# The first half of w_in split later in the head of a linear-attention plus gated-MLP kernel

## Chip, cores and metric

One NeuronCore of a Trainium2 chip runs the whole program; inputs and output lie in HBM. The metric is device microseconds of one execution, the median of several executions. Engines: TensorE (PE), with its weight loads shown apart (PEld); VectorE (DVE); ScalarE (ACT); GpSimd (POOL); SyncE (SP), which only issues DMAs here.

## What is computed

Batch 4, 4 heads of 32, sequence 1088, so a model width of 128; the MLP is 1024 wide and is cut into halves u and v of 512.

```python
q_p, k_p = phi(q), phi(k)            # phi: outer product of two 8-wide projections
kv = einsum('bhsf,bhsd->bhfd', k_p, v); z = k_p.sum(axis=2)
x = (q_p @ kv) / (q_p @ z + 1e-6)    # heads side by side: [B, S, 128]
h = gelu(x @ w_in); u, v = h[..., :512], h[..., 512:]
v_n = layernorm(v) * g_ln
v_s = einsum('ts,bsd->btd', w_sg, v_n) + b_sg[None, :, None]
out = x + (u * v_s) @ w_out
```

`w_in`, `w_out` and S come as 64-bit floats; the chip splits their words into two 32-bit parts itself.

## The kernel before

**Precision.** Most products are made as three matmuls in a 32-bit format that rounds its operands, of a high and a low part of each: high by high, low by high, high by low. So nearly every operand is first copied to a rounded high part (ACT) and then subtracted from itself for the low part (DVE).

**Stages of a batch.** Attention gives x (tiles `x_h`, `x_l`). Then, per 128 rows t of the 9 row tiles: `v1`/`v2` (L746 to L755) multiply x by the second half of `w_in`; `gelu` (L760); mean and variance, for tiles 0 to 2 by `mean`/`sq` on ACT, for the others by `bn` (L776, L777) on DVE; `norm`, a chain of some ten small DVE instructions (L793 to L822); `v3` (L828, ACT) normalizes; `vh` (L838, ACT) and `vl` (L843, DVE) split. The spatial product `z` (L851, L860) sums over t, for 4 blocks db of 128 channels and 3 column parts ci: `zh` is the two matmuls with the high part of W (`w_h`), `zl` the one with its low part (`w_l`). `pu` (L875 to L877) is three matmuls of x by the first half of `w_in`, `ug` (L882) its gelu into u; then `gt`, `gm`, `gh`, `gl`, `po` gate it and multiply by `w_out`.

**The head.** Batch 0 starts with nothing in place, so its stages are written out one by one. While q, k and v arrive, PE makes the features of batch 0 in three column parts c: `qe`, `qm0` (L630), `k2` (L436), `q03` (L650), `den1`, `den2`, `xt` (L668), a transpose `tr` (L686), then `x1` (ACT, L689) and `x2` (DVE, L693) write a third of `x_h`, `x_l`. `fill` steps are matmuls without use (L675). The words of `w_in` are split by `split64` (L241 to L256) in eight steps 0 to 7 per half; `wi1` is the second half (for v), `wi0` the first half (for u). Of `wi0`, step 0 (L241) and 7 (L256, writes `win_h`) run on ACT; 1 (L242), 2 (L245), 3 (L248), 4 (L249), 5 (L250) and 6 (L251, writes `win_l`) on DVE. `wo` is the same for `w_out`; its step 0 (`woa`, L241) waits for the load `raw_out`. `wlo` (L719) subtracts the high part of W from `w_f` for the low one.

**What sets the order.** Every piece of work is a named step. A list `WHEN` of 1773 numbers, written out in the file, gives each step a place; the steps are emitted sorted by place, and each engine runs its own instructions strictly in the order in which they were emitted, with waits on semaphores where the data need them. A step's DMAs go into the queue of the engine that issues it: SP for `load`, POOL for `ld_wh` and `wd`. `gate_wf` (L309) is a one-column POOL copy that reads a chunk of `w_h` and writes into `w_f0`, so that the loads of `w_f` begin only when that chunk of `w_h` has landed.

**Buffers.** `new(shape, tag, name)` takes a place in a ring per tag: tag "x" has 4 (`raw_win1`, `raw_win0`, `x_h`, `x_l`, later `w_f7`, `raw_out`), tag "w" has 8 (`w_f0` to `w_f6`, then the `w_l`). `bank` takes one of 8 PSUM banks; six of them hold z of two channel blocks while the head runs.

Of the kernel before, what the change touches and what calls it, by code (L numbers as in the profile page):

```python
# [9 lines left out]
I64 = mybir.dt.int64  # L10
# [6 lines left out]
P = 128  # L17
# [3 lines left out]
DG = 512  # L21
# [16 lines left out]
HALVES = ((0, 1), (1, 2), (3, 2), (5, 1), (6, 3))  # L38

WHEN = [  # L40
# [111 lines left out]
def tile_kernel(tc, qd, kd, vd, sd, wd, bd, wind, woutd, q0d, vid, outd, pool, dram, psum):  # L152
# [9 lines left out]
    def new(shape, tag, name, dt=F32):  # L162
        return pool.tile(shape, dt, tag=tag, name=name, bufs=BUFS.get(tag, 1))
# [4 lines left out]
    T = {}  # L168
# [140 lines left out]
        G.tensor_copy(w_f(0)[:, :1], f32(T["w_h"][:, HALVES[-2][0], :1]))  # L309

    def load_win(i):
        T["raw_win", i] = new([P, DG], "x", f"raw_win{i}", I64)
        load(T["raw_win", i], wind[:, DG * i : DG * i + DG])

    def load_wout():
# [24 lines left out]
    for p in (1, 0):  # L340
        at(("ld_v0", p), lambda p=p: load_v0(p))
    at("ld_win1", lambda: load_win(1))
    at("ld_win0", lambda: load_win(0))
    at("gate_wh", gate_wh)
    for t, n in HALVES:
# [717 lines left out]
    class Sums:  # L1063
# [28 lines left out]
        def load(self, i):  # L1092
            n, t, k, tag, at = self.PARTS[i]
            if at // 3 not in self.raw:
                self.raw[at // 3] = new([P, 3, WP], "kld", f"wr{at // 3}")
            load(self.of(i), self.d[n][:, t : t + k])
# [322 lines left out]
```

## Time and profile before

| | us |
|---|---|
| runs of the kernel | 319.04, 320.27, 321.16 |
| their median | 320.27 |
| the execution that was profiled | 319.73 |
| its span, first to last instruction | 317.7 |

So 2.0 us of the profiled execution lie around the span. The granted TensorE clock is 1.000 over the span. In the views below a start is in microseconds from the start of the span. A matmul's row gives start and duration; matmuls overlap, so what one costs in a stream is the distance from one start to the next. "x4" is a number of instructions, the arrow a releaser.

### The profile page before, as it was taken

The numbers are of one execution on the slowest core, as the hardware profiler recorded it, in microseconds if no ns is written. First come the engines' busy times: TensorE is split into PE (matmuls) and PEld (weight loads), VectorE is DVE, ScalarE is ACT, GpSimd is POOL, SyncE is SP. The second block draws the span as 40 slices with busy tenths as digits, with TensorE's granted clock in tenths as the row PEclk, the third lists the DMA queues.
The fourth block names the chain that finished last, engine by engine and source line by source line (L and its number), as shares of the span: only waits on it lengthen the run. The fifth ranks groups of instructions, "written<-read, shape, count | busy, mean of one in ns | idle before, by whom it ended". The sixth has DMA issues, their size and how long they took to land.

```text
span 317.7 us, 6545 instructions
## 1 busy us (share of the span) xinstructions
PE 310.8 (98%) x2510; PEld 298.3 (94%) x2510; DVE 271.5 (85%) x654; ACT 163.0 (51%) x360; POOL 35.8 (11%) x52
## 2 busy tenths in 40 slices
PE   7999999999999999999999999999999999999995
PEld 5777999999999999999999999999999999999995
DVE  5899999999998977799798877399888988889675
ACT  4589733556558743454646682345357753334321
POOL 0300000022220001023200002042030000000000
PEclk9999999999999999999999999999999999999999
DMA  6999972556474235642654055724093202510002
GB/s 219 349 425 370 405 313 98 111 123 143 152 172 136 39 109 155 146 129 28 103 94 95 0 153 122 180 66 150 2 200 93 76 18 83 147 47 3 0 0 70
DMA packets 19774, 42.27 MB, mean 133 GB/s; under 512 B 2176, under 2 KB 14624, under 8 KB 19328
## 3 DMA queue, kind: packets, MB, share of 16 engines
q1 hardware_dynamic: 14784, 27.17, 29.6%
q0 software_dynamic: 4960, 14.70, 17.3%
q8 instruction: 19, 0.31, 0.4%
q14 instruction: 11, 0.09, 0.1%
HBM read 35.87 MB, written 8.94 MB: 141 GB/s over the span
## 4 chain that ended last, share of the span: by engine, by line
PE 90%; DVE 6%; DMA 2%; SPq 1%; issue 0%; ACT 0%; DVEq 0%
PE pz L851 33%; PE pz L860 15%; PE pz L1050 5%; PE pu L875 3%; PE pu L877 2%; PE pu L876 2%; PE pv L755 2%; PE pv L747 2%; PE pv L746 2%; PE po L924 2%; PE po L921 2%; PE po L922 2%; DMA vn<-in_q 2%; PE pkv L436 1%; PE pk L404 1%; PE pnd L537 1%
## 5 line engine op out<-in xcount | busy, mean ns | idle before, releaser
L851 PE MATMUL pz<-w_h,vl 128*128 128x362 f32 (+1 forms) x324 | 105.3, 325 | 0.4 <-DVE vl L843 0.4
L851 PE MATMUL pz<-w_h,vh 128*128 128x362 f32 (+1 forms) x324 | 105.3, 325 | 0.0
L860 PE MATMUL pz<-w_l,vh 128*128 128x362 f32 (+1 forms) x288 | 87.5, 325 | 0.0
L851 PEld LDWEIGHTS pz<-w_h,vl 128*128 128x128 f32 x324 | 60.8, 188 | 2.2 <-DVE vl L843 1.2
L851 PEld LDWEIGHTS pz<-w_h,vh 128*128 128x128 f32 x324 | 60.8, 188 | 1.1
L860 PEld LDWEIGHTS pz<-w_l,vh 128*128 128x128 f32 x288 | 53.1, 188 | 0.3
L882 ACT ACTIVATE u<-pu 128x362 f32<-128x362 f32 (+1 forms) x48 | 22.5, 472 | 19.9 <-PE pu L877 12.4
L760 ACT ACTIVATE vn<-pv 128x512 f32<-128x512 f32 x36 | 21.0, 599 | 17.2 <-PE pv L755 16.8
L828 ACT ACTIVATE vn<-vn,nm,rs 128x512 f32<-128x512 f32 x36 | 28.7, 814 | 1.8 <-DVE nm L822 1.4
L888 DVE SCALAR_TENSOR_TENSOR gt<-pz,vi,b_bc 128x362 f32<-128x362 f32 (+3 forms) x41 | 23.5, 581 | 6.1 <-PE pz L851 5.5
L900 ACT CAST gh<-gt 128x362 fp32r<-128x362 f32 (+1 forms) x47 | 22.5, 492 | 12.0 <-DVE gt L895 7.5
L903 DVE TENSOR_TENSOR gl<-gt,gh 128x362 fp32r<-128x362 f32 (+1 forms) x47 | 24.5, 529 | 3.3 <-PE po L922 1.7
L895 DVE TENSOR_TENSOR gt<-gt,u 128x362 f32<-128x362 f32 (+3 forms) x49 | 25.7, 535 | 0.5 <-ACT u L882 0.2
L843 DVE TENSOR_TENSOR vl<-vn,vh 128x128 fp32r<-128x128 f32 (+1 forms) x54 | 22.3, 422 | 3.6 <-ACT vh L838 3.4
L838 ACT CAST vh<-vn 128x128 fp32r<-128x128 f32 (+1 forms) x54 | 20.4, 404 | 8.1 <-PE pz L851 7.7
L776 DVE BATCH_NORM_STATS2 st<-vn 128x6 f32<-128x512 f32 x33 | 22.4, 680 | 1.6 <-ACT vn L760 1.4
L550 DVE RECIPROCAL den<-den 128x362 f32<-128x362 f32 (+1 forms) x9 | 21.7, 2412 | 2.0 <-ACT den L545 1.8
L1050 PE MATMUL pz<-w_h,wb 128*128 128x364 f32 x64 | 19.2, 325 | 0.0
L529 POOL TENSOR_TENSOR qpl<-e_0a,qph 128x362 fp32r<-128x362 f32 x6 | 6.3, 1058 | 107.3 <-ACT qph L524 81.2
L545 ACT ACTIVATE den<-pnd,mask 64x362 f32<-64x362 f32 (+1 forms) x18 | 10.1, 560 | 13.6 <-PE pnd L538 13.4
L875 PE MATMUL pu<-x_h,win_h 128*128 128x362 f32 (+1 forms) x48 | 15.9, 331 | 0.0
L877 PE MATMUL pu<-x_l,win_h 128*128 128x362 f32 (+1 forms) x48 | 15.7, 327 | 0.0
(330 smaller groups left out, 635.8 us busy)
## 6 DMA issues: line engine op xcount, KB each, us to landing
w_f<-in_w SPq DMA_DIRECT2D x9, 576.0 KB
wt<-in_w POOLq DMA_DIRECT2D x6, 768.0 KB, 8.5
w_h<-in_w POOLq DMA_DIRECT2D x2, 1152.0 KB, 8.9
vi<-in_v SPq DMA_DIRECT2D x7, 306.0 KB
w_h<-in_w POOLq DMA_DIRECT2D x1, 1728.0 KB, 14.6
k<-in_k SPq DMA_DIRECT2D x3, 576.0 KB
wt<-wt POOLq DMA_DIRECT2D x2, 768.0 KB, 4.7
out<-o SPq DMA_DIRECT2D x8, 181.0 KB
```

What stands on the lines that cost most here:

```text
L776: V.bn_stats(st, self.vn[:, t])
L828: A.activation(self.vn[:, t], self.vn[:, t], AF.Identity, bias=self.nm[:, t : t + 1], scale=self.rs[:, t : t + 1])
L843: V.tensor_sub(vl[:, ts], self.vn[:, ts, P * db : P * db + P], f32(vh[:, ts]))
L851: mm(self.z[db, ci], lhsT=self.parts[db][i][:, t], rhs=T["w_h"][:, t, AT[ci] : AT[ci] + cw], start=(t == 0 and i == 0), stop=(t == NT - 1 ...
L860: mm(self.z[db, ci], lhsT=self.parts[db][0][:, t], rhs=T["w_l", t][:, AT[ci] : AT[ci] + CH[ci][1]], start=False, stop=False,)
L875: mm(pu, lhsT=T["win_h"][:, ws], rhs=xh[:, cs], start=True, stop=False)
L882: A.activation(self.u[db, ci], self.pu.pop((db, ci)), AF.Gelu_apprx_tanh)
L888: V.scalar_tensor_tensor(self.gt[db, ci][:, s], self.z[db, ci][:, s], T["g_col"][:, db : db + 1], T["b_bc"][:, c0 : c0 + cw][:, s], op0=AL ...
L895: V.tensor_mul(gt, gt, self.u[db, ci][:, s])
L900: A.copy(self.g[db, ci][0], self.gt[db, ci])
L903: V.tensor_sub(self.g[db, ci][1], self.gt.pop((db, ci)), f32(self.g[db, ci][0]))
L1050: mm(self.z[db, ci], lhsT=w[:, i, t % 4], rhs=r[:, cs], start=(t == 0 and q == 0), stop=False)
```

## The change

One line of code and the first third of `WHEN` change. The raw words of the first half (`raw_win0`) take a place in the ring "w" in place of one in "x":

```diff
     def load_win(i):
-        T["raw_win", i] = new([P, DG], "x", f"raw_win{i}", I64)
+        T["raw_win", i] = new([P, DG], "x" if i else "w", f"raw_win{i}", I64)
         load(T["raw_win", i], wind[:, DG * i : DG * i + DG])
```

```diff
 WHEN = [
-    1, 7, 2, 0, 5, 6, 8, 10, 15, 18, 21, 24, 56, 59, 66, 72, 76, 80, 35, 38, 9, 12, 14, 11, 13, 16, 17, 19, 20, 22,
+    1, 7, 2, 0, 5, 6, 8, 10, 15, 18, 21, 24, 56, 59, 66, 93, 97, 102, 35, 38, 9, 12, 14, 11, 13, 16, 17, 19, 20, 22,
...
```

The lists were sorted to see the order they make. Places 0 to 66 and all from 522 on hold the same steps in the same order; those between are permuted. No step is added or taken out, and no instruction of one changes. Places of the steps that matter (before, after):

| step | before | after |
|---|---|---|
| `wi0` 0, 1, 2, 3 | 103, 105, 109, 118 | 98, 113, 117, 127 |
| `wi0` 7, 4, 5, 6 | 115, 130, 116, 137 | 238, 247, 257, 276 |
| `pu` and `ug` of (db 0, ci 0) | 150, 158 | 319, 354 |
| `pu` and `ug` of (0, 1) | 172, 202 | 365, 402 |
| `pu` and `ug` of (0, 2) | 214, 217 | 290, 320 |
| `pu` of (1, 0) | 218 | 282 |
| first `zh` (0, 2, t 0), (0, 0, t 0), (0, 1, t 0) | 209, 211, 205 | 186, 187, 205 |
| `bn` 3, 4, 5 | 196, 178, 206 | 191, 190, 182 |
| `vl` of t 0 | 204 | 185 |
| `x1` of c 1, c 2; `gelu` 5 | 129, 175; 194 | 135, 164; 159 |
| `v1` 3, 6, 7, 8 | 136, 181, 183, 189 | 165, 166, 179, 192 |
| `v2` 3, 6, 7, 8 | 156, 193, 197, 199 | 175, 178, 201, 198 |
| `ld_wh` 3, 5, 6; `gate_wf` | 72, 76, 80; 142 | 93, 97, 102; 110 |
| `ld_w` 0; `ld_wout`; `ld_b`; `ld_v` of batch 1 | 145; 180; 201; 207, 210 | 114; 162; 281; 308, 324 |
| `wo` 0, `v3` 6, `vh` 6, `v3` 7, `vh` 7 | 275, 287, 291, 293, 299 | 251, 274, 291, 283, 285 |
| `zh` (0, 0, t 6) | 313 | 294 |
| `k1`, first `kf`, `k2` of batch 1 | 396, 410, 428 | 397, 411, 420 |

On SP the 124 DMAs stand in the same order before and after. On POOL two subtractions of batch 1 change places (`ql` 0 and 1), and nothing else does.

## Rows read from the trace of the kernel before

**Rows 1.** The page, part 1 (busy time) and part 4 (chain that ended last).
```profile
PE 310.8 (98%) x2510; PEld 298.3 (94%) x2510; DVE 271.5 (85%) x654; ACT 163.0 (51%) x360; POOL 35.8 (11%) x52
...
PE 90%; DVE 6%; DMA 2%; SPq 1%; issue 0%; ACT 0%; DVEq 0%
```

**Rows 2.** Busy time by stretch: PE, PEld, DVE, ACT, POOL, clock, DMA share, GB/s.
```profile
24.00:32.00 8.00, 7.55 (x38) 5.65 (x36) 7.59 (x36) 7.55 (x18) 0.68 (x1) 1.00 0.98 365
32.00:40.00 8.00, 8.00 (x50) 7.87 (x49) 7.46 (x29) 5.89 (x13) 0.00 (x0) 1.00 1.04 407
40.00:48.00 8.00, 8.00 (x50) 7.63 (x49) 8.00 (x11) 2.54 (x6) 0.00 (x0) 1.00 0.76 296
```

**Rows 3.** Timeline of PE at the first spatial products: start, duration, instruction, idle before.
```profile
28.06 0.33 PE L851 MATMUL pz<-w_h,vh 128*128 128x362 f32 x1
28.79 0.43 PE L851 MATMUL pz<-w_h,vl 128*128 128x362 f32 x1 [0.41 <-DVE vl L843]
...
33.07 0.32 PE L851 MATMUL pz<-w_h,vh 128*128 128x364 f32 x1
33.23 0.33 PE L851 MATMUL pz<-w_h,vl 128*128 128x364 f32 x1
```

**Rows 4.** Timeline of PE, 23 to 26 us: products for v, and u's between them.
```profile
22.71 0.40 PE L747 MATMUL pv<-win_l,x_h 128*128 128x512 f32 x1
22.94 0.39 PE L746 MATMUL pv<-win_h,x_h 128*128 128x512 f32 x1
...
24.92 0.33 PE L875 MATMUL pu<-x_h,win_h 128*128 128x362 f32 x1
25.09 0.33 PE L876 MATMUL pu<-x_h,win_l 128*128 128x362 f32 x1
25.26 0.33 PE L877 MATMUL pu<-x_l,win_h 128*128 128x362 f32 x1
25.57 0.50 PE L746 MATMUL pv<-win_h,x_h 128*128 128x512 f32 x1
```

**Rows 5.** Chain that ended last, 19 to 29 us: start, duration, what.
```profile
19.04 0.33 DVE wi0g L250
...
21.11 0.60 DVE wi0a L249
...
21.83 0.60 DVE win_l L251
...
25.87 0.61 DVE st L776
...
28.54 0.21 DVE vl L843
28.75 0.04 issue
28.79 1.08 PE pz L851 x5
```

**Rows 6.** Waits, 0 to 60 us: engine, line, what it waited for; total, times, longest.
```profile
POOL w_f L309 <- DMA w_h<-in_w: 9.9, 1, 9.9
...
ACT woa L241 <- DMA raw_out<-in_w_out: 1.6, 1, 1.6
```

**Rows 7.** Timeline of SP: DMA issues.
```profile
23.53 3.44 SPq L300 DMA_DIRECT2D w_f<-in_w  x5
27.09 0.42 SPq L317 DMA_DIRECT2D raw_out<-in_w_out  x1
```

**Rows 8.** Timelines of ACT from the landing of raw_out, and of DVE.
```profile
37.98 0.67 ACT L241 ACTIVATE woa<-raw_out 128x512 f32<-128x512 f32 x1 [1.55 <-DMA raw_out<-in_w_out]
38.55 0.82 ACT L828 ACTIVATE vn<-vn,nm,rs 128x512 f32<-128x512 f32 x1
39.40 0.30 ACT L838 CAST vh<-vn 128x128 fp32r<-128x128 f32 x1
39.60 0.81 ACT L828 ACTIVATE vn<-vn,nm,rs 128x512 f32<-128x512 f32 x1
...
38.15 0.29 DVE L843 TENSOR_TENSOR vl<-vn,vh 128x128 fp32r<-128x128 f32 x1
```

**Rows 9.** Timeline of PE round tile 6 of the first channel block.
```profile
43.06 0.32 PE L851 MATMUL pz<-w_h,vh 128*128 128x362 f32 x1
43.22 0.32 PE L851 MATMUL pz<-w_h,vl 128*128 128x362 f32 x1
43.38 0.32 PE L851 MATMUL pz<-w_h,vh 128*128 128x362 f32 x1
43.69 0.43 PE L851 MATMUL pz<-w_h,vl 128*128 128x362 f32 x1
43.96 0.33 PE L851 MATMUL pz<-w_h,vh 128*128 128x364 f32 x1
```

**Rows 10.** Timeline of PE: batch 1's keys, and the same for batch 2.
```profile
55.40 1.21 PE L404 MATMUL pk<-sk,k 128*32 128x64 f32 x72
56.54 0.43 PE L860 MATMUL pz<-w_l,vh 128*128 128x362 f32 x1
...
59.33 1.73 PE L436 MATMUL pkv<-vi,kp 128*32 128x34 f32 x144
60.99 0.43 PE L851 MATMUL pz<-w_h,vh 128*128 128x362 f32 x1
...
118.08 1.49 PE L436 MATMUL pkv<-vi,kp 128*32 128x34 f32 x144
```

**Rows 11.** Timeline of DVE, the features of batch 1's keys.
```profile
56.98 3.07 DVE L210 TENSOR_TENSOR kp<-pk,kb 128x256 f32<-128x256 f32 x9
```

**Rows 12.** Timeline of PE, first 20 us: the engine at its two clock levels.
```profile
0.94 3.25 PE L202 MATMUL warm<-ones 128*64 128x64 f32 x28 [0.94 <-POOL ones L194]
...
8.21 1.56 PE L610 MATMUL pn<-vn,sk 128*128 128x384 f32 x4 [0.86 <-DMA vn<-in_q]
9.31 2.19 PE L621 MATMUL pab<-qs,ex 128*128 128x384 f32 x8
```

78 rows, old and new, of the table WHEN are left out of this document.

## Prediction, made before the changed kernel was run

> **What bounds the kernel now.** Read first the busy shares and the chain that ended last: PE is busy for 98% of the span and 90% of that chain is PE's own work [rows 1]. The change takes no matmul away and adds none, so the time can move only by PE's gaps. The stretches say where these are: none of 8 us between 32 and 48, 0.45 us between 24 and 32, where DVE (7.59 of 8) and ACT (7.55) are as full as PE [rows 2]. A busy PE is not quite a streaming one, so the third view is PE's own timeline, read start to start. In a stream one matmul of 362 columns follows the next after 0.16 us (33.07 to 33.23); at the first spatial product it is 0.73 us (28.06 to 28.79), released by DVE's `vl`, so 0.57 us are lost there [rows 3]. Smaller losses stand at 43.4 us (0.31 and 0.27 us in place of 0.16, 0.26 us lost) [rows 9] and in the keys of batch 1: their 144 matmuls last 1.73 us, those of batch 2 last 1.49, so 0.24 us are lost [rows 10]. The named losses are 1.07 us together. What the change can win is of this order, and it has to be won twice: at the first spatial product, and at each later place where PE waits for something that does not depend on the head.
>
> **First place: what DVE no longer does before the first spatial product.** The chain up to it is DVE without a pause. Behind it go steps 4, 5 and 6 of `wi0`: 0.60, 0.33 and 0.60 us [rows 5], 1.53 us in all. Of the three `bn` steps before `vl`, two go behind and one comes ahead, so one of 0.61 us goes [rows 5]. Together 2.14 us: if DVE were alone, the low part of the first pair, at 28.79 us now, could start at 26.65.
>
> PE must be ready for it too. Six matmuls of `pu` also go behind; they are 0.165 us apart (24.92, 25.09, 25.26) [rows 4], so 0.98 us of PE work leave this stretch. In the old order three of them run right before the product with the last third of x (`v1` 6, at 25.57 us) [rows 4]: they cover the wait for that third. It comes over ACT (`x1`), where one `ug` leaves the queue ahead of it and one `gelu` (step 5) joins it, so I expect the third no sooner than 0 to 0.5 us before its old time, `v1` 6 at 25.1 to 25.6. What is late next, then, is PE itself: `v1` 6, `v2` 3, `v2` 6, `v1` 7, six matmuls at 0.23 us (22.71 to 22.94) [rows 4], 1.4 us, end at 26.5 to 27.0. The low part of the first pair starts at about 27.2 us. PE is 1.6 us earlier there, with 0.98 us of `pu` and three matmuls of `v` (`v1` 8 twice, `v2` 7 and `v2` 8: four, 0.93 us) still to do. Bounds: 26.65 us (all of DVE's saving arrives), 28.79 us (none). I take 27.2, nearest to the row of `v1` 6.
>
> **Second place: tile 6, which hangs on a DMA.** ACT stands still for 1.6 us until `raw_out` has landed, and everything behind that wait in its queue stands too [rows 6, 8]. Behind `wo` 0 in both orders come the normalizing and splitting of tiles 6 to 8, so these cannot begin before 38.55 us, however fast the head is. Does the landing move? SP's 124 DMAs keep their order; the loads of `w_f` wait for the gate, a POOL copy that itself waits 9.9 us for a chunk of `w_h` [rows 6]; POOL's queue up to the gate is the same, so moving `gate_wf` and three `ld_wh` in the list moves nothing, and `ld_wout` follows five loads of `w_f` with no pause (23.53 plus 3.44, then 27.09) [rows 7]. So the landing stays at 37.9, and the place for `raw_win0` in the ring "w" buys no earlier load. It costs nothing either: that ring has eight places for `raw_win0` and `w_f0` to `w_f6`, and the first `w_l` finds `raw_win0` read.
>
> The new order puts `v3` 6, `v3` 7, `vh` 7 ahead of `vh` 6. From 38.55: two `v3` of 0.8 us, a `vh` of 0.2, then `vh` 6 takes 0.30 [rows 8]: done at about 40.65, the first matmul of `zh` (0, 0, t 6) at 40.7; `vl` 6 takes 0.29 us after `vh` 6 [rows 8], so the second matmul starts at 41.0. When does PE get there? Between the low part of the first pair and this place the new order has 73 matmuls at 0.16 and four at 0.23 us [rows 3, 4], 12.7 us: from 27.2 it arrives at 39.9, from 26.65 at 39.4, and only from later than 28.0 does it arrive after 40.7. So PE waits 0.8 us there for a landing; the gain of the first place is spent.
>
> Now the same point of work in the old order. There `zh` (0, 0, t 6) starts at 43.06 us [rows 9], with 18 matmuls done that the new order has still to do (six of `pu`, twelve of `zh`): 18 x 0.1615 = 2.91 us, so its equivalent is 40.15. The new order stands at 40.7, 0.55 us behind, and the wait for `vl` 6 between the two matmuls adds 0.15 us net of what it overlaps: 0.7 us behind. The old order loses its 0.26 us at 43.4 only afterwards; the new one has then had tiles 6 to 8 long enough not to. Net: 0.45 us behind.
>
> **Third place: batch 1's keys.** After `k1` PE needs cover while DVE makes nine features, 3.07 us [rows 11], before the last third of `k2`. The old order gives 2.79 us (56.54 to 59.33) [rows 10]; the new one has 22 matmuls, 3.55 us, between them, and DVE's queue ahead of the features is shorter by two `gm`, a `gt` and a `wo` step against a `vl` and a `gm`. So the 0.24 us lost there [rows 10] go. Bounds: all of them, or nothing.
>
> **Everything else at nothing.** The three `wi0` steps moved behind, 1.53 us, run in a DVE stretch that has 0.54 us free (7.46 of 8 between 32 and 40) [rows 2]; what has no room delays the subtractions `wlo`, which PE needs from 45 us on and DVE makes up to 51; if that cover is gone it costs up to 1.0 us. `ug` now waits for a place in its ring of three on ACT, which is idle for two thirds of 40 to 48 [rows 2]. From place 522 on the order is the old one.
>
> **Sum.** Against the profiled execution: 319.73 + 0.45 - 0.24 = 319.94 us. That execution lies 0.54 us under the median of the runs shown, so in their measure 320.27 + 0.21 = 320.5 us. About 1% (3.2 us) is what a measurement of this kernel can tell from no change; the forecast is no change.
>
> **Rivals.**
> *The gain is kept (faster).* If PE need not wait at tile 6 (the landing comes 1.5 us sooner, or other work is in place), the first pair at 26.65 carries through: 39.4 against 40.15, less 0.26 and 0.24, is 1.25 us gained: 319.0. For it: the unbroken DVE chain [rows 5]. Against: ACT's wait names the DMA [rows 6, 8], and nothing in front of that DMA moves.
> *The cover is gone (slower).* `pu` filled PE while the last third of x came; if that third, and so the first pair, is no sooner than now, PE idles for the 0.98 us of `pu` and the matmuls of `v`. First pair at 28.79: tile 6 is reached at 41.5, 1.36 us behind the old order, less 0.26 and 0.24: 0.86 us slower, and with 1.0 us of delayed `wlo` 1.9: 321.1 to 322.1. It decides once the first pair comes after 28.0 us. For it: ACT is nearly as full as DVE there (7.55 of 8) [rows 2]. Against: 2.14 us of DVE work leave the chain.
> *The clock falls back.* PE's granted clock is at the 2.4 GHz level after the first 9 us: four matmuls of 384 columns took 1.56 us before, eight took 2.19 after [rows 12], and the gap of 0.73 us at 28.06 [rows 3] left it there (1.00 in the stretch [rows 2]). If longer gaps sent it to 1.2 GHz for as long as at the start, 0.94 to 9.3 us, half of 8.4 us is lost: 324.7. The Trainium skill (TensorE: Matmul & The Clock Gate, "HAM oscillation — how this bites in real kernels") says that a matmul kernel with idle gaps falls back to the half clock; by that rule taking `pu` out of a waiting stretch is the wrong way. The gaps I expect are under 1 us, near one that did no harm.
>
> **Chances.** The forecast 0.55 (its own range 319.6 to 321.3: 0.2 to 0.7 us behind, and half a microsecond of spread as between the runs shown), gain kept 0.22, cover gone 0.20, clock 0.03. The first three lie within 1% of 320.27 (317.07 to 323.47); faster by over 1% would need three times the named losses. Within 1%: 0.94, faster 0.03, slower 0.03. Range 318.8 to 322.0.
>
> **What would show it.** Right: first `vl` matmul at 26.6 to 28; `woa` still at 38.0 after a longer wait than 1.6 us; a PE gap at 40 to 41 us released by `vh` or `vl`; the keys of batch 1 near 1.5 us; PEclk 1.00. Wrong: `raw_out` landing at another time, no PE gap at 40 to 41, a first pair after 28, or a span off by more than 1.5 us.

## The result: 4 us slower, spread over the whole kernel

| | before | after |
|---|---|---|
| median (lowest to highest), 6 runs each | 319.79 us (319.04 to 321.16) | 323.84 us (322.90 to 324.73) |
| ratio, 95% interval | | 1.011 (1.0088 to 1.0131) |
| profiled execution; its span | 319.73; 317.7 us | 324.73; 322.8 us |

The medians lie 4.05 us apart; by the interval the change costs 2.8 to 4.2 us. The prediction was 320.5 us, so some 3.3 us are to be explained. Read the page first: busy time and the chain, which answer to [rows 1], and the three costliest groups of part 5 (behind the bar: busy us, mean ns of one; behind the second bar: idle us of the engine before them).

```profile
PE 316.8 (98%) x2510; PEld 303.7 (94%) x2510; DVE 272.5 (84%) x654; ACT 163.3 (51%) x360; POOL 35.3 (11%) x52
...
PE 93%; DVE 2%; ACT 2%; DMA 1%; SPq 0%; issue 0%; DVEq 0%
...
L851 PE MATMUL pz<-w_h,vh 128*128 128x362 f32 (+1 forms) x324 | 106.4, 328 | 0.0
L851 PE MATMUL pz<-w_h,vl 128*128 128x362 f32 (+1 forms) x324 | 106.4, 328 | 0.0
L860 PE MATMUL pz<-w_l,vh 128*128 128x362 f32 (+1 forms) x288 | 88.1, 328 | 0.0
```

The same 2510 matmuls keep PE busy for 316.8 us in place of 310.8 [rows 1], and PE waits for nothing ahead of these three groups: their last column is 0.0, where time lost to a wait would stand. Over the whole span PE is not busy for 6.0 us, 6.9 before. What grew is the matmul itself. Before, the three groups read:

```profile
L851 PE MATMUL pz<-w_h,vl 128*128 128x362 f32 (+1 forms) x324 | 105.3, 325 | 0.4 <-DVE vl L843 0.4
L851 PE MATMUL pz<-w_h,vh 128*128 128x362 f32 (+1 forms) x324 | 105.3, 325 | 0.0
L860 PE MATMUL pz<-w_l,vh 128*128 128x362 f32 (+1 forms) x288 | 87.5, 325 | 0.0
```

325 to 328 ns looks like nothing, and neighbours overlap, so a mean duration is not what a matmul costs. The cost is the distance from start to start. The last 1745 matmuls stand in the same order in both kernels. The first and the last row of this part, before:

```profile
77.32 0.32 PE L851 MATMUL pz<-w_h,vh 128*128 128x362 f32 x1
...
313.61 0.47 PE L928 MATMUL pl<-gt,wout_f 128*128 128x180 f32 x2
```

and after:

```profile
78.76 0.32 PE L851 MATMUL pz<-w_h,vh 128*128 128x362 f32 x1
...
318.31 0.47 PE L928 MATMUL pl<-gt,wout_f 128*128 128x180 f32 x2
```

The new order enters this part 1.44 us late and takes 3.26 us longer for it (239.55 us in place of 236.29). Behind 200 us, well inside it, stand 65 products of these three groups with nothing between them. The first and the last of them on PE's timeline, before:

```profile
202.43 0.32 PE L851 MATMUL pz<-w_h,vh 128*128 128x362 f32 x1
...
212.75 0.32 PE L851 MATMUL pz<-w_h,vl 128*128 128x364 f32 x1
```

and after:

```profile
205.47 0.32 PE L851 MATMUL pz<-w_h,vh 128*128 128x362 f32 x1
...
216.07 0.32 PE L851 MATMUL pz<-w_h,vl 128*128 128x364 f32 x1
```

64 steps take 10.32 us before and 10.60 after: 161.3 and 165.6 ns a step. The 936 products of the three groups at 4.4 ns more each would be 4.1 us (an estimate). Not every stretch is as bad as this one, so a second measure takes them all: over every matmul of 362 or 364 columns that is followed by the next within 0.2 us, the distance less 0.160 us, summed. I call it the excess: 3.76 us before, 7.50 after. The difference, 3.74 us, is nearly all of the 4.05; 2.65 us of it stand at the three groups. It is read from one execution of each kernel.

What had changed for a matmul some 125 us behind the last moved step? Its operands' places in SBUF. A ring of buffers gets its address when its tag is first used, in the order of those first uses. Before, the first `bn` (place 178) opens the ring "st", 2 places of 32 bytes, ahead of the first `vh` (185). After, `vh` stands at 181, ahead of the first `bn` (182). So the 64 bytes of "st" come to lie behind the rings of `vh` and `vl` in place of ahead of them, and all four buffers (two of each) lie 64 bytes lower. From the compiled kernels' allocation, bytes within a partition:

```
            before                     after
w_h         13600  (256*n + 32)        13600  (256*n + 32)
w_l ring   163616  (256*n + 32)       119840  (256*n + 32)
vh         201056  (256*n + 96)       200992  (256*n + 32)
vl         210272  (256*n + 96)       210208  (256*n + 32)
```

The ring of `w_l` moved too, by the one changed line of code, but to a place that is the same within 256 bytes. Other buffers moved as well; what they do to the pace was not tried one by one. `vh` and `vl` are the stationary operands, `w_h` and `w_l` the moving ones.

### The profile page after: what moved, and what is told of

The parts are those of the page before. It is cut to its first block, busy times and chain, and to the rows that moved or that the text cites. A ratio compares the mean times of both kernels' runs of the same rounds, so it can differ in the third digit from the quotient of the medians.

```text
span 322.8 us, 6549 instructions
## 1 busy us (share of the span) xinstructions
PE 316.8 (98%) x2510; PEld 303.7 (94%) x2510; DVE 272.5 (84%) x654; ACT 163.3 (51%) x360; POOL 35.3 (11%) x52
## 4 chain that ended last, share of the span: by engine, by line
PE 93%; DVE 2%; ACT 2%; DMA 1%; SPq 0%; issue 0%; DVEq 0%
PE pz L851 34%; PE pz L860 15%; PE pz L1050 5%; PE pu L875 3%; PE pu L876 2%; PE pu L877 2%; PE pv L755 2%; PE pv L746 2%; PE pv L747 2%; PE pkv L436 2%; PE po L921 2%; PE po L924 2%; PE po L922 2%; PE pk L404 2%; DMA k<-in_k 1%; PE pnd L536 1%
## 5 line engine op out<-in xcount | busy, mean ns | idle before, releaser
L851 PE MATMUL pz<-w_h,vh 128*128 128x362 f32 (+1 forms) x324 | 106.4, 328 | 0.0
L851 PE MATMUL pz<-w_h,vl 128*128 128x362 f32 (+1 forms) x324 | 106.4, 328 | 0.0
L860 PE MATMUL pz<-w_l,vh 128*128 128x362 f32 (+1 forms) x288 | 88.1, 328 | 0.0
L851 PEld LDWEIGHTS pz<-w_h,vh 128*128 128x128 f32 x324 | 61.2, 189 | 1.8 <-DVE gt L888 0.3
L851 PEld LDWEIGHTS pz<-w_h,vl 128*128 128x128 f32 x324 | 61.0, 188 | 1.5 <-DVE vl L843 0.3
L860 PEld LDWEIGHTS pz<-w_l,vh 128*128 128x128 f32 x288 | 53.3, 188 | 0.1
L903 DVE TENSOR_TENSOR gl<-gt,gh 128x362 fp32r<-128x362 f32 (+1 forms) x47 | 25.3, 545 | 3.6 <-PE po L922 1.8
L776 DVE BATCH_NORM_STATS2 st<-vn 128x6 f32<-128x512 f32 x33 | 22.4, 678 | 1.8 <-ACT vn L760 1.7
L876 PE MATMUL pu<-x_h,win_l 128*128 128x362 f32 (+1 forms) x48 | 15.8, 329 | 0.0
```

The lines of the kernel that those rows point to most:

```text
L776: V.bn_stats(st, self.vn[:, t])
L851: mm(self.z[db, ci], lhsT=self.parts[db][i][:, t], rhs=T["w_h"][:, t, AT[ci] : AT[ci] + cw], start=(t == 0 and i == 0), stop=(t == NT - 1 ...
L860: mm(self.z[db, ci], lhsT=self.parts[db][0][:, t], rhs=T["w_l", t][:, AT[ci] : AT[ci] + CH[ci][1]], start=False, stop=False,)
L876: mm(pu, lhsT=T["win_l"][:, ws], rhs=xh[:, cs], start=False, stop=False)
L903: V.tensor_sub(self.g[db, ci][1], self.gt.pop((db, ci)), f32(self.g[db, ci][0]))
```

## Experiments

Times are compared with runs of the kernel before on the same chip. Theory A: the place of `vh` and `vl`. B: the place of the ring of `w_l`. C: the order of the steps itself.

**The new order with `vh` and `vl` put back.**

```diff
-                const("pad_v", [P, 32])
+                const("pad_v", [P, 48])
```

> The changed kernel with 64 bytes more of padding ahead of the tiles vh and vl, which puts these four back on the SBUF addresses that they have in the kernel before (vh0 at 201056 bytes of a partition in place of 200992); W's low parts stay where the change put them, and the order is the changed one. Theory A (the change moved vh and vl, the operands that PE loads as weights, by 64 bytes, and each matmul of the stream follows the last one some 3.5 ns later for it): distance of two matmuls of 362 columns back to 160 to 162 ns from 164.5, time 319.5 to 320.8 us, ratio 1.000 to 1.003. Theory B (the address of the ring of W's low parts does it): nothing comes back, 323 to 324.5 us. Theory C (the new order itself costs the 4 us, by gaps): 323 to 324.5 us.

Measured: 320.65 us against 319.84, ratio 1.0025 (1.0008 to 1.0042). The stretch of 65 takes 10.33 us again:

```profile
204.17 0.33 PE L851 MATMUL pz<-w_h,vh 128*128 128x362 f32 x1
...
214.50 0.32 PE L851 MATMUL pz<-w_h,vl 128*128 128x364 f32 x1
```

64 bytes of padding give 3.2 us back. The rest, 0.8 us (0.3 to 1.3), is what the order costs at most, and this was what the prediction was about (+0.2). For 0.35 us of it the excess is still higher than before (4.11 less 3.76); half of that stands at the products of `kv` (L536 to L538), whose buffers the padding moved by 64 bytes.

**The old order with `vh` and `vl` 64 bytes lower.**

```diff
-                const("pad_v", [P, 32])
+                const("pad_v", [P, 16])
```

> The kernel before, its order and rings untouched, with 64 bytes less of padding ahead of vh and vl, so that they lie where the changed kernel has them. Theory A: distance of two matmuls of 362 columns 164 to 165 ns, 322.8 to 324 us, ratio 1.010 to 1.013. Theories B and C: as before, 319.5 to 320.3 us, ratio 0.998 to 1.002.

Measured: 323.01 us, ratio 1.0096 (1.0076 to 1.0117); the stretch takes 10.53 us (204.98 to 215.51). No step moved, and 3.2 us are lost. A is shown from both sides. The padding moves the rings behind `vh` and `vl` too (`gt`, `o`, `kv`); two of the runs below, with `vh` alone and with `w_h` alone moved, leave those where they were.

**The old order with the changed line of code alone.**

```diff
-        T["raw_win", i] = new([P, DG], "x", f"raw_win{i}", I64)
+        T["raw_win", i] = new([P, DG], "x" if i else "w", f"raw_win{i}", I64)
```

> The kernel before with the one line of code of the change alone: the raw words of w_in's first half in the ring of W, the order untouched. The ring of W moves to the changed kernel's addresses (119840 on), vh and vl stay on those of before. Theory A: as before, 319.5 to 320.5 us, ratio 0.998 to 1.002. Theory B: 322.5 to 324 us, ratio 1.009 to 1.013, the distance of L860's matmuls above all at 165 ns. Theory C: as before.

Measured: 320.22 us, ratio 1.0011 (0.9988 to 1.0035), stretch 10.32 us. B falls.

**The new order with `vh` and `vl` 128 bytes higher than the change put them.**

```diff
-                const("pad_v", [P, 32])
+                const("pad_v", [P, 64])
```

> The changed kernel with 128 bytes more of padding ahead of vh and vl: 64 bytes beyond their addresses of before (vh0 at 201120). Theory A in the form that the place within 128 bytes decides: the same place as in the changed kernel, so 164.5 ns a matmul and 323 to 324.5 us. Theory A in the form that another period decides: anything between 319.5 and 324.5. Theories B and C: 323 to 324.5 us.

Measured: 323.93 us, ratio 1.0129 (1.0109 to 1.0149), stretch 10.59 us. As slow as after: the cause is neither the step of 64 bytes as such nor being below the old place.

The next five ask which operand it is, and what a good place is.

**`vl` alone, and `vh` alone, moved.** The two buffers are made in two statements with 64 bytes of padding between; for the second run `pad_v` is 16 as well. In the first the rings behind `vl` move along; in the second nothing moves but the ring of `vh`.

```diff
-                self.parts[db] = [new([P, NT, P], f"v{i}", f"v{i}{self.b}_{db}", F32R) for i in "hl"]
+                self.parts[db] = [new([P, NT, P], "vh", f"vh{self.b}_{db}", F32R)]
+                if "pad_v2" not in T:
+                    const("pad_v2", [P, 16])
+                self.parts[db].append(new([P, NT, P], "vl", f"vl{self.b}_{db}", F32R))
```

> The kernel before with the low parts (vl) alone moved by 64 bytes a partition, from 210272 to 210336; the high parts stay at 201056. Theory A1 (each weight operand costs by its own place): of 936 products of a group with three weight reads for each column chunk (vh by w_h, vl by w_h, vh by w_l) a third has vl, so about a third of the 3.2 to 3.7 us that moving both cost comes back, 1.1 to 1.3 us: 320.9 to 321.2 us; the line that multiplies vh with w_l (L860) keeps its distance of 161 ns or is late only by what its neighbours are, and the line that alternates vh and vl (L851) rises about half way, to 163. Theory A2 (what counts is how vh and vl lie to each other): moving one alone costs as much as moving both did not, or nothing: 319.8 or over 323.

> The kernel before with the high parts (vh) alone moved by 64 bytes, from 201056 to 200992; the low parts stay at 210272. Theory A1: two thirds of the 3.2 to 3.7 us, 2.1 to 2.5 us, so 321.9 to 322.3 us; L860 at the full 165 ns, L851 about half way at 163. Theory A2: the same time as the run with vl alone moved.

Measured: `vl` alone 323.91 us, ratio 1.0126 (1.0091 to 1.0161); `vh` alone 323.04, ratio 1.0083 (1.0061 to 1.0105). The stretch with `vl` alone moved (the line is L854 here) takes 10.59 us:

```profile
204.54 0.33 PE L854 MATMUL pz<-w_h,vh 128*128 128x362 f32 x1
...
215.13 0.32 PE L854 MATMUL pz<-w_h,vl 128*128 128x364 f32 x1
```

A1 falls: it gave `vl` a third of the loss, and `vl` alone costs all of it. One operand out of place slows its neighbours too. Averaged over all pairs of the trace, a product of `w_l` and `vh` followed by one of `w_h` and `vh` is 165.2 ns long here (160.7 before), though none of the four operands in it moved. Only where two products of `w_l` and `vh` follow each other is the distance as before (162.0 and 161.8 ns). A2 has the right size for `vl` alone, but by it moving both together would cost nothing, and that run was as slow. For `vh` alone A1 had 321.9 to 322.3, which is too low as well.

**`vh` and `vl` 32 bytes lower; `w_h` alone 64 bytes higher; `vh` and `vl` 128 bytes lower.**

```diff
-                const("pad_v", [P, 32])
+                const("pad_v", [P, 24])
```

> The kernel before with vh and vl both moved by 32 bytes, vh to 201024, which is a multiple of 128 plus 64 (before: plus 96; after: plus 32). If only the half of the 128 bytes counts (the upper half fast, the lower slow): as before, 319.8 to 320.3, distances of 161. If the place 32 alone is bad because the other operand w_h lies at 32 as well: also as before. If 96 is the one good place: between, 321 to 323, distances of 163 to 165.

```diff
-        const("w_h", [P, NT, SW], F32R)
         const("pad", [P, 16])
+        const("w_h", [P, NT, SW], F32R)
```

> The kernel before with the spatial weight w_h alone moved by 64 bytes, from 13600 (a multiple of 128 plus 32) to 13664 (plus 96, where vh and vl lie); its low part w_l and vh, vl stay. Theory R (the two operands of one product get in each other's way when they lie at the same place within 128 bytes): the line with w_h (L851) rises to 164.5 ns and more, the line with w_l (L860) stays at 161, two thirds of 3.2 to 3.7 us: 321.9 to 322.3 us. Theory A (the place of vh and vl alone): 319.8 to 320.3 us and both lines at 161.

```diff
-            if "pad_v" not in T:
-                const("pad_v", [P, 32])
```

> The kernel before without the 128 bytes of padding ahead of vh: vh and vl move by exactly 128 bytes, vh to 200928, again a multiple of 128 plus 96. Theory R2 (the two operands of a product must lie 64 bytes apart within 128; w_h and w_l lie at plus 32): nothing changes, 319.8 to 320.4 us, distances of 161 ns. Rival (the pattern repeats only every 256 bytes or more, or any shift harms): 322.5 to 324 us, distances of 164 to 167 ns.

Measured: 32 bytes 323.01 us, ratio 1.0093 (1.0060 to 1.0126); `w_h` alone 324.32 us, ratio 1.0125 (1.0100 to 1.0150); 128 bytes 323.10 us, ratio 1.0073 (1.0045 to 1.0101). The second is the telling one: `vh` and `vl` lie where they were good, and moving the other operand costs as much as the change did.

```profile
205.65 0.33 PE L851 MATMUL pz<-w_h,vh 128*128 128x362 f32 x1
...
216.25 0.33 PE L851 MATMUL pz<-w_h,vl 128*128 128x364 f32 x1
```

10.60 us. So the place of `vh` by itself is not the cause; how the operands lie to each other is part of it. R had the direction, but two thirds of the loss. Its expectation that L860, whose `w_l` did not move, would stay fast holds only where two of its products follow each other (161.4 ns); beside a product with `w_h` they are slow (167.9). The first run says that 32 bytes are enough to lose it. The third says that the pattern does not repeat every 128 bytes, against R2.

**The new order, `vh` and `vl` as the change put them, `w_h` and `w_l` moved instead.** `pad` goes ahead of `w_h` as above; 64 bytes go ahead of the ring of `w_l` and leave `pad_w`, so that `vh` stays. The buffers between these two places move along.

```diff
+        if i == 0:
+            const("pad_q", [P, 16])
         T["raw_win", i] = new([P, DG], "x" if i else "w", f"raw_win{i}", I64)
...
-            const("pad_w", [P, 40])
+            const("pad_w", [P, 24])
```

> The kernel after with vh and vl left where the change put them (plus 32 within 128 bytes), and w_h and w_l moved by 64 bytes instead, to plus 96. Theory R2 (only how the operands lie to each other counts): distances of 161 ns again and the time of the run that moved vh and vl back, 320.3 to 321.0 us. Rival (vh and vl have a bad place of their own): distances of 164 ns or more and 323.5 to 324.5 us.

Measured: 324.02 us, ratio 1.0100 (1.0054 to 1.0147), excess 7.24 us. R2 falls here too. (The stretch of 65 alone, 10.39 us, would have told otherwise; this is why the excess of all products stands beside it.)

**`vh` and `vl` 256 bytes higher; all four operands 64 bytes higher.** The first has `pad_v` at 96. The second has `pad` ahead of `w_h` and `pad_w` at 56, and `vh` and `vl` follow.

> The kernel before with vh and vl moved by 256 bytes, vh from 201056 to 201312. R3 (vh and vl must lie 64 bytes behind w_h and w_l within 256 bytes) and S with a period of 256: as before, 319.6 to 320.6 us, distances of 161 ns. If the pattern has a longer period or the one place alone is good: 322.4 to 324 us, distances of 164 to 167 ns.

> The kernel before with w_h, w_l, vh and vl all moved by 64 bytes: w_h to 13664 and vh to 201120, where each of them alone was slow (w_h there: 324.3 us; vh there in the new order: 323.9 us). R3 (only how they lie to each other within 256 bytes counts): as before, 319.6 to 320.6 us, distances of 161 ns. S (the places count by themselves): 323 to 325 us, distances of 164 ns and more.

Measured: 256 bytes 320.08 us, ratio 1.0004 (0.9981 to 1.0026), stretch 10.32 us, excess 3.81: as before. All four moved: 322.00 us, ratio 1.0049 (1.0020 to 1.0078), between what R3 and S had forecast; excess 5.65, and the stretch is good, though `vh` and `w_h` lie where each was slow alone:

```profile
203.40 0.33 PE L851 MATMUL pz<-w_h,vh 128*128 128x362 f32 x1
...
213.74 0.32 PE L851 MATMUL pz<-w_h,vl 128*128 128x364 f32 x1
```

10.34 us. Over the whole trace the products of 362 columns have 162.0 ns (L851) and 161.6 (L860), against 161.1 and 160.9 before and 164.5 and 165.6 after. So about three quarters (L851) and more (L860) of their loss come back. Of the 1.9 us of excess that are left, 0.6 stand at products of the last batch's tiles `wb` (L1012 to L1014, whose sum over 160 ns goes from 0.12 to 0.71 us), 0.55 at those of `vh` and `vl` themselves, and 0.3 each at `pu` and at `po` (L921 to L924), none of whose operands moved. S falls for the products of `vh` and `vl`, R3 holds for most of them and not for all.

All of it together, places within 256 bytes; stretch and excess are of one execution of each kernel, the ratio is of all runs:

```
run                        w_h  w_l   vh   vl   65 products   excess   ratio to before
before                      32   32   96   96   10.32 us      3.76 us
ring line alone             32   32   96   96   10.32         3.81     1.0011
vh, vl 256 higher           32   32   96   96   10.32         3.81     1.0004
new order, vh, vl back      32   32   96   96   10.33         4.11     1.0025
all four 64 higher          96   96  160  160   10.34         5.65     1.0049
vh, vl 128 lower            32   32  224  224   10.56         6.47     1.0073
vh, vl 32 lower             32   32   64   64   10.50         6.68     1.0093
vh alone 64 lower           32   32   32   96   10.54         7.04     1.0083
new order, w_h, w_l higher  96   96   32   32   10.39         7.24     1.0100
old order, vh, vl 64 lower  32   32   32   32   10.53         7.47     1.0096
after                       32   32   32   32   10.60         7.50     1.0110
vl alone 64 higher          32   32   96  160   10.59         7.68     1.0126
new order, vh, vl at 160    32   32  160  160   10.59         8.13     1.0129
w_h alone 64 higher         96   32   96   96   10.60         8.26     1.0125
```

The excess over 3.76 us follows the time in every row, to 0.7 us. What the first five rows, with the good stretch, share is `vh` and `vl` 64 bytes behind `w_h` and `w_l` within 256. Both at a distance of 0, 32, 128 or 192 bytes are slow.

**The new order, put back, without the wait for `raw_out`.** Two steps of `wo` stand ahead of tiles 6 to 8 in ACT's and DVE's queue. In the run with `vh` and `vl` put back that wait was 3.87 us long. ACT's timeline of that run:

```profile
38.72 0.67 ACT L241 ACTIVATE woa<-raw_out 128x512 f32<-128x512 f32 x1 [3.87 <-DMA raw_out<-in_w_out]
```

PE stood for it, at tile 6's first product:

```profile
39.69 0.32 PE L877 MATMUL pu<-x_l,win_h 128*128 128x364 f32 x1
41.38 0.43 PE L851 MATMUL pz<-w_h,vh 128*128 128x362 f32 x1 [1.37 <-ACT vh L838]
```

The edit, in the list of places (`pad_v` stays at 48):

```diff
 order of steps:
-  wo 0    (place 251, ahead of v3 6)
-  wo 3    (place 287, ahead of vl 7)
+  wo 0    (behind vh (1, 2))
+  wo 3    (behind vl (1, 2))
```

> The kernel after with vh and vl moved back by 64 bytes, as in the run of that kind, and with the two steps that wait for raw_out moved: ScalarE's (wo 0) from ahead of tile 6's v3 to behind the last copy of vh before the pair of (1, 2), VectorE's (wo 3) to behind that pair's vl. If the wait for raw_out is what holds tile 6 (TensorE stood 1.37 us ahead of tile 6's first product in the run without this move, ScalarE 3.87 us in its wait): that gap goes, 1.0 to 1.4 us are saved, 319.2 to 319.7 us, at or below the kernel before. If the tile is late for other reasons, or the raw words then hold up something behind: no change, 320.4 to 321 us.

Measured: 319.92 us against 320.16, ratio 0.9988 (0.9968 to 1.0008). The gap is gone from PE's timeline:

```profile
39.76 0.33 PE L877 MATMUL pu<-x_l,win_h 128*128 128x364 f32 x1
39.93 0.33 PE L851 MATMUL pz<-w_h,vh 128*128 128x362 f32 x1
```

and ACT reaches `woa` behind its tiles, with no wait:

```profile
40.11 0.67 ACT L241 ACTIVATE woa<-raw_out 128x512 f32<-128x512 f32 x1
```

The places of the four operands are those of the run without this edit, and so are stretch (10.33 us) and excess (4.09). Against that run 0.37% or 1.2 us are won: an estimate from the two ratios, whose intervals allow 0.4 to 2 us. It is the best form of the change that was tried, and the interval does not set it apart from the kernel before.

## Why the prediction was wrong, and where it was right

**The step that failed** is its first: "The change takes no matmul away and adds none, so the time can move only by PE's gaps." Every later number kept 0.16 us for a matmul [rows 3] as a constant of the work. It depends on the work and on where the operands lie: 161.3 ns before and 165.6 after, in the stretch of 65 products. With that, "everything else at nothing" and "it costs nothing either" of the place in the ring "w" asked only whether a place is free in time, and "from place 522 on the order is the old one" took the old pace for granted there. The ring line did turn out free (ratio 1.0011); the reorder of `bn` and `vh` was not. The table of places above has the `bn` steps and leaves out the one that mattered beside them, the first `vh` (185, then 181). The paddings `pad_v`, `pad_w` and `pad` in the code were there to be asked about. The size: 3.2 us of the 4.05, read twice (putting the place right in the new order, and wrong in the old). One sign that the prediction gave for being wrong came true at once, a span off by more than 1.5 us (322.8 against 317.7); a second did too, no PE gap at 40 to 41 us, as told below.

**The first place was right.** `v1` 6 was forecast at 25.1 to 25.6 us and came at 25.23; the low part of the first pair was forecast at 27.2 and came at 27.64, in the two runs of the new order with the place put right at 26.61 and 26.67, at the lower bound of 26.65. That bound was itself 0.18 us too late: two `bn` steps, not three, stood before `vl`, and the one that goes is two instructions, 0.61 us (L776) [rows 5] and 0.18 (L777, at 26.51 in the same chain). (Why the pair is 1 us later in the changed kernel's execution is not shown; a few slower products are not enough.) After:

```profile
27.32 0.32 PE L851 MATMUL pz<-w_h,vh 128*128 128x364 f32 x1
27.64 0.43 PE L851 MATMUL pz<-w_h,vl 128*128 128x364 f32 x1
```

The 0.57 us lost between these two before [rows 3] are 0.16 now (0.32 less 0.16). Some of it stands ahead of them instead: PE loses 0.47 us at 25.8 us, at the products for v that wait for the last third of x.

**The second place was right in kind, but the wait shows only with the operands put right.** `woa` waits for `raw_out` as in [rows 8], 2.47 us long in place of 1.55, since ACT reaches it 0.55 us sooner (35.88 in place of 36.43) and the landing comes 0.37 us later. Tile 6's first product came at 41.05 (forecast 40.7), the second at 41.37 (41.0):

```profile
38.35 0.69 ACT L241 ACTIVATE woa<-raw_out 128x512 f32<-128x512 f32 x1 [2.47 <-DMA raw_out<-in_w_out]
...
41.05 0.42 PE L851 MATMUL pz<-w_h,vh 128*128 128x362 f32 x1
41.37 0.43 PE L851 MATMUL pz<-w_h,vl 128*128 128x362 f32 x1
```

PE barely waits here (0.17 us from the matmul before), since it gets there later: its first pair came later than forecast, and its products are slower. With the place put right it comes to the tile at 39.85 us (39.69 and one distance), as forecast (39.9), and stands 1.5 us in place of 0.8, for the landing was 0.7 us later in that execution (38.72). Moving the two steps took the gap away, so this wait held the tile. Of the order's 0.8 us the forecast had the sign and the place; its price, 0.2 us, lies below what was measured (0.3 to 1.3).

**The third place was right.** Batch 1's second run of keys takes 1.49 us, as batch 2's did before, and not 1.73 [rows 10]:

```profile
61.33 1.49 PE L436 MATMUL pkv<-vi,kp 128*32 128x34 f32 x144
62.75 0.43 PE L851 MATMUL pz<-w_h,vh 128*128 128x364 f32 x1
```

**The rivals.** The gain kept (1.25 us faster without the wait at tile 6) did not come, for the wait was there; with it taken away the order is 0.4 us faster than before, between 1.0 faster and 0.3 slower, so a gain of 1.25 us is not shown. The cover gone is not what happened: the first pair came before 28.0. The clock did not fall (1.000), though 324.7 us was the number nearest to the result: a right size from a wrong cause. Its price has no row to stand on either: the profile before has a granted clock of 1.00 from 4.2 to 9.0 us too, and read start to start the matmuls of 384 columns in [rows 12] take 0.28 us each ahead of 9.31 us (8.21 to 9.31 for four) and 0.27 behind it (9.31 to 11.44 for eight). The durations of 1.56 and 2.19 us were taken for two clock levels. The row that follows those of [rows 12]:

```profile
11.44 2.29 PE L436 MATMUL pkv<-vi,vn 128*64 128x34 f32 x72
```

## What to carry to other kernels

A reorder can change every instruction's operands without changing an instruction: where buffers are placed by first use, as here, compare the address lists of both kernels before counting steps. When a kernel is slower everywhere by a little, measure start-to-start distances in a stretch that the change did not touch; here gaps did not show it (0.0) and mean durations hardly did (325 to 328 ns). An edit meant for the order should be timed with the old addresses held by padding, else two effects are read as one.

## What the runs showed that was not expected

The pace of a stream of matmuls depends on where its operands lie in SBUF: for 362 columns at the same granted clock (1.00) 161 to 162 ns (means of L851 and L860) where the stretch is good and 163.5 to 166.9 in the others, with the same instructions. The layout is good again when `vh` and `vl` move by 256 bytes, and not by 32, 64 or 128. One operand out of place slows the products beside it that don't use it. The Trainium skill (SBUF — State Buffer, "Who interferes with whom") gives TensorE two independent read ports, one for the moving operand and one for loading the weights, and says that it never waits on anyone. The section is about engines that get in each other's way and has nothing on where operands lie. These runs show a dependence that it does not lead one to expect: moving `w_h` alone, which TensorE reads only as the moving operand, cost 1.25%. The mechanism was not found; no run tells whether TensorE's two reads disturb each other or other engines' accesses have a part in it. R3 (64 bytes behind, within 256) fits all the rows but one: with all four operands moved alike 0.5% remained, a third of it in products none of whose operands moved. A distance of 96 bytes was not tried, and neither were other places of `wb`.
